# Block-sparse attention and a Fourier mixer on one core: mask matmuls regrouped and used for the second batch, late value sums and earlier q, k turned by VectorE

## The chip, the core and the metric

The kernel runs on one core of a Trainium2 chip. The metric is the time of one execution on the device in microseconds (us), lower is better. A program's time here is the median of its runs. TensorE is PE in the profile, VectorE is DVE, ScalarE is ACT, GpSimd is POOL and SyncE, which only issues transfers here, is SP. Each engine works through its own queue in order.

## What is computed

The first stage is attention with a block mask over 4 batches, 8 heads, 768 positions and head size 64; its result, laid out as (batch, position, head and feature), feeds a Fourier mixing layer with two dense products.

```python
scores = (q @ k.T) / sqrt(64)
scores = where(mask, scores, -1e9)            # 32 x 32 blocks: neighbours, first and last, 3 drawn per row
attn   = exp(scores - max) / sum
x      = (attn @ v) as (4, 768, 512)
u      = x + real(fft(fft(x, over positions), over features))
un     = (u - mean(u)) / sqrt(var(u) + 1e-6)
out    = u + relu(un @ w_ch1) @ w_ch2          # w_ch1 512 x 2048, w_ch2 2048 x 512
```

The weights arrive as 64-bit floats and are rounded to 32 bits on the chip.

## The kernel before, in words

**Units, slots, phases.** Two heads make a pair, so a batch has four pairs and the kernel sixteen, numbered n from 0. A pair has twelve units: two halves of the queries (384 each) times six chunks c of 128 keys. A slot is two units, so a pair has six slots (s from 0 to 5) and a batch 24, called a phase. `slot(sl)` at line 1240 writes out one slot by hand, and the order of the calls is the order on every queue: scores and exp of this slot's two units, values of the last slot's, then small pieces, then pieces of the mixer. There are 96 slots and one to finish.

**Scores.** `scores` (line 533) makes the scores of both heads of one unit, keys on the partitions, as two matmuls with 64 rows each, one per half of the array. In the first batch (n < NP = 4) two more matmuls with 24 rows in bf16 add the mask straight behind each unit: `of_k` says to which of the 24 blocks a key belongs, `off_q` which blocks a query may not see. In later batches the mask is a table `mask` of bytes instead, made once by matmuls in `mask_step` during phase 0.

**Exp and mask.** `weigh` (line 551) takes exp on ACT. In the first batch it writes `e` to SBUF; later it writes back to PSUM, and DVE multiplies by the mask (line 562). From the second batch on GpSimd sums the weights over the chunks into `acc` (line 572); in the first batch TensorE does it in `add_up` (line 618). Score tiles `ps_s` have two buffers, weight tiles `e` four.

**Values.** `values` (line 575) accumulates the products with v in one PSUM bank (`ps_o`, one buffer) over the six chunks of a half; ACT copies the result to `oT` (line 591, one buffer), and `place` (line 595) turns it by three TensorE transposes and lets ACT copy it into the pair's 128 columns of `x`.

**q and k.** Features must lie on the partitions. Up to pair 8 `turn` (line 469) does it with six TensorE transposes for q and six for k through the one bank `ps_t`, with ACT copies (lines 486 and 492; for pair 0's second half of q the copies are DVE's) and a square for a later range test. From pair 9 = `BY_VECTOR` on, `load_blocks` (line 214) loads 32 x 32 blocks so that block transposes of DVE (`flip_blocks`, line 511) finish the turn; ACT then puts q in order (`in_order`, line 520).

**Mixer.** `mixer` (line 872) gives, for each batch, steps that run apart (normalise, fold, Fourier products, statistics), then the late work: products in seven-multiplication form (`quad`) and second dense products (`channels`). `begin(b)` queues the batch's steps in the second slot of the next phase; `gap` issues a step where a planner with fixed costs per engine (`when`, `busy`) holds it ready; late work fills the slots, and `until` works it off where a buffer of `x` is needed again. With no late work queued, nothing but ready steps fills TensorE.

**Weights.** `w_load` and `w_round` bring 32 chunks through six rotating rooms (`room(0)` to `room(5)`) in phase 0, 1.42 chunks a slot: two ACT and five DVE instructions each.

**Small pieces.** `short` holds turns, places and sums that wait for a bank; the loop at line 1301 takes them in the slot, in phase 0 all that are ready. At the end of a slot come the DVE turns, then `load_q(n + 2)` in s = 3 and `load_k(n + 1)` in s = 0 (lines 1314 to 1317), then weights and tables.

Of the kernel before, what the change touches and what calls it, by code (L numbers as in the profile page):

```python
# [11 lines left out]
FP32 = mybir.dt.float32  # L12
# [90 lines left out]
def kernel(  # L103
# [88 lines left out]
    def busy(engine, us, after=0.0):  # L192
        when[engine] = max(when[engine], after) + us
        return when[engine]
# [14 lines left out]
    loaded, v_of = {}, {}  # L209


    BY_VECTOR = 2 * NP + 1

    def load_blocks(n, a, tile):

# [110 lines left out]
    at_k = acc_p.tile([P, 2, 2 * HS], BF16, tag="acc", name="at_k")  # L326
    at_q = acc_p.tile([P, 2, 2 * HS], BF16, tag="acc", name="at_q")
    of_k, off_q, keep_q = at_k[:, 0, :], at_q[:, 0, :], at_q[:, 1, :]

    def twice(t):  # L330
        nc.vector.tensor_copy(out=t[D:D + NB, :], in_=t[0:NB, :])
# [131 lines left out]

    turned, e_of, acc_of, o_of, sums_of, x_of, sp_of = {}, {}, {}, {}, {}, {}, {}
    s_at, e_at, oT_at, acc_at = {}, {}, {}, {}

# [61 lines left out]
    UNITS = len(pairs) * UP  # L530
    SLOT = 2

    def scores(u):
        n, w = divmod(u, UP)
        half, c = divmod(w, C)
        qT, kT = turned[n, 0], turned[n, 1]
        s = ps_s.tile([P, 2, 512], FP32, tag="s", name="s")
        busy("PE", 0.72 if n >= NP else 1.0, max(e_at.get(u - SLOT, 0.0), z_at[u % 2]))
        s_at[u] = when["PE"] + HOP
        for i in range(2):  # L540
            nc.tensor.matmul(s[:, i, 0:HS], kT[D * i:D * i + D, c * P:(c + 1) * P],  # L541
                             qT[D * i:D * i + D, half * HS:(half + 1) * HS],
                             start=True, stop=n >= NP)
        if n < NP:
            for i in range(2):
                nc.tensor.matmul(s[:, i, 0:HS], of_k[D * i:D * i + NB, c * P:(c + 1) * P],
                                 off_q[D * i:D * i + NB, half * HS:(half + 1) * HS],
                                 start=False, stop=True)
        return s

    def weigh(u, s):
        n, w = divmod(u, UP)
        half, c = divmod(w, C)
        e = ep.tile([P, 2, HS], FP32, tag="e", name="e")
        e_of[u] = e
        if n < NP:
            nc.scalar.activation(out=e, in_=s[:, :, 0:HS], func=ACT.Exp, scale=scale)
            e_at[u] = busy("ACT", 0.8, s_at[u]) + HOP
            return
        nc.scalar.activation(out=s[:, :, 0:HS], in_=s[:, :, 0:HS], func=ACT.Exp, scale=scale)  # L560
        m = mask[:, c, half * HS:(half + 1) * HS].rearrange("p (o s) -> p o s", o=1)
        nc.vector.tensor_tensor(out=e, in0=s[:, :, 0:HS], in1=m.broadcast_to([P, 2, HS]),  # L562
                                op=ALU.mult)
        e_at[u] = busy("DVE", 0.97, busy("ACT", 0.8, s_at[u]) + HOP) + HOP
        if c > 0:
            acc_at[n, half] = busy("POOL", 2.0, e_at[u]) + HOP
        if c == 1:
            acc_of[n, half] = acc_p.tile([P, 2, HS], FP32, tag="acc", name="acc")

        for i in range(2 if c > 0 else 0):  # L570
            acc = acc_of[n, half][:, i, :]
            nc.gpsimd.tensor_add(out=acc, in0=e_of[u - 1][:, i, :] if c == 1 else acc,  # L572
                                 in1=e[:, i, :])

    def values(u):
        n, w = divmod(u, UP)
        half, c = divmod(w, C)
        e = e_of[u]
        busy("PE", 0.75, e_at[u])
        vt = v_of[n]  # L580
        if c == 0:
            o_of[n, half] = ps_o.tile([P, HS], FP32, tag="o", name="o")
        o = o_of[n, half]
        for i in range(2):
            nc.tensor.matmul(o[D * i:D * i + D, :], vt[:, i, c, :], e[:, i, :],  # L585
                             start=(c == 0), stop=(c == C - 1))
        if c == C - 1:
            if half == 1:
                v_of.pop(n)
            oT = sum_p.tile([P, HS], FP32, tag="oT", name="oT")  # L590
            nc.scalar.copy(out=oT, in_=o_of.pop((n, half)))
            oT_at[n, half] = busy("ACT", 0.5, when["PE"] + HOP) + HOP
            o_of[n, half] = oT

    def place(n, half):

        b, j = pairs[n]
        oT = o_of.pop((n, half))
        if j == 0:
            x_of[b, half] = xp.tile([P, T, DM], FP32, tag=("xA", "xB")[half], name="x")  # L600
        xt, at = ps_t.tile([P, 512], FP32, tag="t", name="xt"), bank("t")
        for c in range(T):
            nc.tensor.transpose(xt[:, c * P:(c + 1) * P], oT[:, c * P:(c + 1) * P], ident)  # L603
        nc.scalar.copy(out=x_of[b, half][:, :, j * P:(j + 1) * P],
                       in_=xt[:, 0:HS].rearrange("p (c f) -> p c f", c=T))
        give(at, busy("ACT", 0.5, busy("PE", 0.45, oT_at[n, half]) + HOP))

    def into_sums(key, j, sp):
        if j == 0:
# [610 lines left out]
    def begin(b):  # L1220


        before, after, rest = mixer(b, x_of[b, 0], x_of[b, 1])
        any_of = len(late) + len(apart) + 4 * len(rest)
        hold = 2 * T
        apart.extend((*step, any_of) for step in norm_steps(b) + before)
        apart.extend((*step, hold) for step in after)
        apart.append(("-", lambda: late.extend(rest), 0.0, 0.0, 0.0, hold))

    def w_loads():  # L1230
        while state["got"] < min(len(wchunks), state["w"] + ROOMS):
# [8 lines left out]
    def slot(sl):  # L1240
# [1 line left out]
        n, s = divmod(sl, SP)  # L1242
        units = range(SLOT * sl, SLOT * sl + SLOT)
        if sl < B * SB:
            for u, ps in [(u, scores(u)) for u in units]:
                weigh(u, ps)
        if not late:
            gap(1.5)
        if 0 < sl <= B * SB:
            done = [u - SLOT for u in units]  # L1250
            for u in done:
                values(u)
            if phase == 0 or sl == SB:
                add_up(done)
            for u in done:
                e_of.pop(u)

        reuse = n % NP == 0 and phase >= 2
        if sl > 0 and s == (5 if reuse else 3) and sl <= B * SB:
            b, j = pairs[n]  # L1260
            at = oT_at[n, 0]
            if reuse:
                until(lambda: (b - 2, 0) in finished)
                at = when["PE"] + LEAVES
            short.append(("t", at, lambda: place(n, 0)))
        if 0 < sl <= B * SB and s == 0 and n % NP != 1:
            short.append(("t", oT_at[n - 1, 1], lambda: place(n - 1, 1)))
        if sl < B * SB and n % NP == 1 and s == 1:
            b = pairs[n - 1][0]
            at = oT_at[n - 1, 1]  # L1270
# [29 lines left out]

        while short and (s in (2, 5) or len(short) > 1 or phase == 0 or r == 0):
            ready = [i for i in short if max(i[1], min(free[i[0]])) <= when["PE"] + 0.1]
            if not ready and s not in (2, 5) and r > 0:
                break
            item = ready[0] if ready else short[0]
            short.remove(item)
# [1 line left out]
        if BY_VECTOR <= n + 1 < len(pairs):  # L1308
            for at, fn, args in ((0, squares, (n + 1, 0)), (1, flip_blocks, (n + 1, 0)),
                                 (2, in_order, (n + 1,)), (4, flip_blocks, (n + 1, 1)),  # L1310
                                 (5, squares, (n + 1, 1))):
                if s == at:
                    fn(*args)
        if s == 3 and n + 2 < len(pairs):
            load_q(n + 2)
        if s == 0 and 0 < n < len(pairs) - 1:
            load_k(n + 1)
        w_loads()
        w_steps(sl)
        if sl >= 4 and sl % 2 == 0:  # L1320
            table_step()

# [139 lines left out]
```

## Time and profile before

| what | us |
|---|---|
| median of 14 runs | 1110.6 |
| lowest, highest | 1106.49, 1112.19 |
| the profiled execution's own time | 1111.29 |
| its span in the trace | 1109.5 |

| phase 0 slots | from 9.3 to 136.1 us of the span |
|---|---|
| phase 1 slots | 136.1 to 253.2 |
| first batch's late work begins | about 282 |
| phases 2 and 3 | 253 to 838 |
| last batch's rest | 838 to 1109 |

The page gives busy time by engine, the span in slices, the chain of work that ended last, and groups of instructions. In a line of the timeline the first number is the start, the second the time until the last of the merged instructions ends, and x4 the number of them; matmuls overlap in the pipeline, so the cost of one is read from start to next start. A float32 matmul shows as two records, so the four records of one unit's scores are two matmuls. In the view of stretches each row has the length and then the busy time of PE, PE's weight loads, DVE, ACT and POOL, each with its count, then the granted clock of TensorE (1.00 is full), the share of the transfer engines and GB/s.

### The profile page before, as it was taken

Reading aid. Unit: us, or ns where it says so; the run is one execution under the profiler, and the core shown is the slowest. Engines: PE = TensorE matmul, PEld = TensorE weight load, DVE = VectorE, ACT = ScalarE, POOL = GpSimd, SP = SyncE. Lnnn points to the kernel's source line nnn. Section 1 sums busy time; section 2 is a strip of 40 time slices with the busy share of each in tenths; the row PEclk is TensorE's granted clock in tenths of the full one; section 3 lists DMA queues with packets and bytes.
Section 4 is the critical chain, followed back from the end, with each engine's and each line's share of the span. In section 5 each row is a group of like instructions: output and inputs, shape, how many; then the busy total and the mean of one; then the engine's idle time right before and its main releaser. Section 6 shows DMA issues by size and latency. Waiting matters only on the chain.

```text
span 1109.5 us, 12273 instructions
## 1 busy us (share of the span) xinstructions
PE 1065.7 (96%) x4370; PEld 537.9 (48%) x4370; DVE 670.8 (60%) x1227; ACT 389.6 (35%) x786; POOL 271.0 (24%) x302
## 2 busy tenths in 40 slices
PE   7999988998899999999999999999999999999996
PEld 3333333543545545444444545444444555568675
DVE  5688878497864535564558635555456446575563
ACT  4788855465202102253443112344330202120210
POOL 1000079487200001245537000343540000000000
PEclk9999999999999999999999999999999999999998
DMA  8557422022000000212210000211000000100001
GB/s 229 149 161 238 113 51 64 15 44 43 1 1 1 1 1 18 62 23 41 43 29 15 0 1 1 55 45 29 1 1 1 0 1 20 38 1 1 1 16 44
DMA packets 86689, 44.28 MB, mean 40 GB/s; under 512 B 74318, under 2 KB 79452, under 8 KB 86620
## 3 DMA queue, kind: packets, MB, share of 16 engines
q1 hardware_dynamic: 84732, 42.62, 14.6%
q10 hardware_dynamic: 1856, 0.79, 0.3%
q8 instruction: 36, 0.59, 0.2%
q14 instruction: 33, 0.27, 0.1%
q0 software_dynamic: 32, 0.01, 0.0%
HBM read 37.11 MB, written 6.29 MB: 39 GB/s over the span
## 4 chain that ended last, share of the span: by engine, by line
PE 82%; DVE 10%; ACT 2%; issue 2%; DMA 1%; POOL 1%; SPq 0%; ACTq 0%; DVEq 0%; POOLq 0%
PE y L1017 23%; PE z L961 14%; PE s L541 10%; PE o L585 8%; PE yp L961 7%; PE yy L1080 6%; PE xp L961 3%; DVE e L562 3%; PE zp L774 1%; PE sp L632 1%; PE zp L745 1%; DMA out_dram<-x 1%; PE xt L603 1%; DVE wraw L457 1%; DVE w_sb L452 1%
## 5 line engine op out<-in xcount | busy, mean ns | idle before, releaser
L572 POOL TENSOR_TENSOR acc<-acc,e 128x384 f32<-128x384 f32 x192 | 197.2, 1060 | 89.5 <-DVE e L562 88.8
L541 PE MATMUL s<-qT,kT 64*128 64x384 f32 x768 | 164.2, 531 | 15.2 <-DVE e L562 11.0
L562 DVE TENSOR_TENSOR e<-s,mask 128x768 f32<-128x768 f32 x144 | 131.1, 949 | 65.0 <-ACT s L560 63.0
L585 PE MATMUL o<-e,vr 128*64 128x384 f32 x768 | 148.2, 508 | 0.0
L560 ACT ACTIVATE s<-s 128x768 f32<-128x768 f32 x144 | 109.5, 792 | 89.2 <-PE s L541 87.8
L1020 DVE TENSOR_TENSOR x<-y,x 128x512 f32<-128x512 f32 x72 | 49.8, 692 | 146.5 <-PE y L1017 146.5
L1017 PE MATMUL y<-w_sb,hA 128*128 128x512 f32 x288 | 129.5, 596 | 1.1 <-ACT zs L776 1.1
L1017 PE MATMUL y<-w_sb,hB 128*128 128x512 f32 x288 | 128.5, 596 | 1.0 <-DVE x L1020 1.0
L572 POOL TENSOR_TENSOR acc<-e 128x384 f32<-128x384 f32 x48 | 50.0, 1062 | 232.2 <-DVE e L562 190.0
L541 PEld LDWEIGHTS s<-qT,kT 64*128 64x128 f32 x768 | 62.3, 187 | 85.1 <-DVE e L562 38.0
L966 DVE TENSOR_TENSOR hA<-z,hA 128x384 f32<-128x384 f32 x64 | 35.7, 558 | 97.4 <-PE z L961 97.4
L961 PE MATMUL z<-unT,t 128*128 128x384 f32 x256 | 93.0, 486 | 0.0
L837 POOL TENSOR_SCALAR st<-st 128x1 f32<-128x1 f32 x24 | 6.6, 276 | 348.2 <-DVE st L836 347.7
L1017 PEld LDWEIGHTS y<-w_sb,hB 128*128 128x128 f32 x288 | 53.4, 190 | 67.3 <-issue 65.6
L585 PEld LDWEIGHTS o<-e,vr 128*64 128x64 f32 x768 | 47.5, 139 | 75.9 <-issue 72.3
L1017 PEld LDWEIGHTS y<-w_sb,hA 128*128 128x128 f32 x288 | 52.9, 190 | 62.9 <-issue 58.5
L970 ACT ACTIVATE hA<-hA 128x384 f32<-128x384 f32 x64 | 33.5, 523 | 119.9 <-DVE hA L966 119.5
L961 PEld LDWEIGHTS z<-unT,t 128*128 128x128 f32 x256 | 48.7, 190 | 33.9
L970 ACT ACTIVATE hB<-hB 128x384 f32<-128x384 f32 x64 | 33.5, 523 | 86.1 <-DVE hB L966 86.1
L961 PE MATMUL xp<-unT,w_sb 128*128 128x384 f32 x128 | 48.6, 503 | 1.3 <-DVE x L1020 0.7
L981 ACT COPY hA<-xp 128x384 f32<-128x384 f32 x32 | 15.3, 478 | 95.8 <-PE xp L961 95.8
L961 PE MATMUL z<-t,w_sb 128*128 128x384 f32 x128 | 46.6, 487 | 0.9 <-DVE t L923 0.9
(197 smaller groups left out, 1409.7 us busy)
## 6 DMA issues: line engine op xcount, KB each, us to landing
wraw<-in_moe_w_ch_dram SPq DMA_DIRECT2D x32, 512.0 KB
vr<-in_v_dram SPq DMA_DIRECT2D x30, 192.0 KB
qr<-in_q_dram SPq DMA_DIRECT2D x48, 64.0 KB
kr<-in_k_dram SPq DMA_DIRECT2D x14, 192.0 KB
qb<-in_q_dram SPq DMA_DIRECT2D x28, 96.0 KB
kb<-in_k_dram SPq DMA_DIRECT2D x28, 96.0 KB
out_dram<-x SPq DMA_DIRECT2D x16, 128.0 KB
out_dram<-x SPq DMA_DIRECT2D x8, 256.0 KB
```

The source lines that it names most:

```text
L541: nc.tensor.matmul(s[:, i, 0:HS], kT[D * i:D * i + D, c * P:(c + 1) * P], qT[D * i:D * i + D, half * HS:(half + 1) * HS], start=True, stop ...
L560: nc.scalar.activation(out=s[:, :, 0:HS], in_=s[:, :, 0:HS], func=ACT.Exp, scale=scale)
L562: nc.vector.tensor_tensor(out=e, in0=s[:, :, 0:HS], in1=m.broadcast_to([P, 2, HS]), op=ALU.mult)
L572: nc.gpsimd.tensor_add(out=acc, in0=e_of[u - 1][:, i, :] if c == 1 else acc, in1=e[:, i, :])
L585: nc.tensor.matmul(o[D * i:D * i + D, :], vt[:, i, c, :], e[:, i, :], start=(c == 0), stop=(c == C - 1))
L961: nc.tensor.matmul(to, a[:, k, :], c[:, k, :], start=(k == 0), stop=(k == ND // 2 - 1))
L966: tt(out=to, in0=ps, in1=a, op=ALU.add)
L970: nc.scalar.activation(out=h, in_=h, func=ACT.Relu)
L981: nc.scalar.copy(out=h11, in_=x)
L1017: nc.tensor.matmul(y, hs[0, half][:, l, m * P:(m + 1) * P], w2_sb[:, 4 * r + l, :], start=(l == 0), stop=(l == 3))
L1020: nc.vector.tensor_tensor(out=x[:, m, :], in0=y, in1=x[:, m, :], op=ALU.add)
L1080: nc.tensor.matmul(ps, a[:, k, :], c[k // 2][:, k % 2, :] if isinstance(c, list) else c[:, k, :], start=(k == 0), stop=(k == 3))
```

## The change

Four parts.

1. `scores` takes both units of a slot: first the score matmuls of both, then the mask matmuls of both, on all 64 rows of each half of the array; the rows beyond the 24 of `of_k` and `off_q` are set to zero by two memsets.
2. Units of later batches use mask matmuls too as long as `factors["at"]` is set: `keep_factors` copies both factors by two transfers into `room(2)` in slot 21, and the step that queues the first batch's late work ends it. For these units exp writes `e`, and DVE's multiply is left out.
3. `BY_VECTOR` becomes 5, so pairs 5 to 8 are loaded in blocks and turned by DVE.
4. For pairs 9 to 11 and 13 to 15, DVE's block transpose takes the value sums from PSUM to `oT`, and sixteen transfers of 32 partitions x 3 x 32 elements put each half into `x`, with no TensorE transpose and no ACT copy.

Besides, the loads of q and k are issued earlier in their slot, and slot 1 no longer leaves its second turn (the second half of pair 0's q) to slot 2.

```diff
-    BY_VECTOR = 2 * NP + 1
+    BY_VECTOR = NP + 1
...
+    nc.vector.memset(of_k, 0.0)
+    nc.vector.memset(off_q, 0.0)
...
+    by_pe = set()
+    factors = {"at": (of_k, off_q)}
+    def keep_factors():
+        kept = room(2, [P, 2, S], "factors", BF16)
+        for a, t in enumerate(factors["at"]):
+            nc.sync.dma_start(out=kept[:, a, :], in_=t)
+        factors["at"] = kept[:, 0, :], kept[:, 1, :]
...
+    def scores(us):
+        for u in us:
+            s = ps_s.tile([P, 2, 512], FP32, tag="s", name="s")
+            if n < NP or (factors["at"] and True):
+                by_pe.add(u)
+            for i in range(2):
+                rows = slice(D * i, D * i + D)
+                nc.tensor.matmul(s[:, i, 0:HS], kT[rows, c * P:(c + 1) * P], qT[rows, queries],
+                                 start=True, stop=u not in by_pe)
+        for u, s in got:
+            if u not in by_pe:
+                continue
+            for i in range(2):
+                rows = slice(D * i, D * i + D)
+                nc.tensor.matmul(s[:, i, 0:HS], at_k[rows, c * P:(c + 1) * P], at_q[rows, queries],
+                                 start=False, stop=True)
...
     def weigh(u, s):
-        if n < NP:
+        if u in by_pe:
             nc.scalar.activation(out=e, in_=s[:, :, 0:HS], func=ACT.Exp, scale=scale)
...
     def values(u):
-            nc.scalar.copy(out=oT, in_=o_of.pop((n, half)))
+            if in_blocks(n):
+                nc.vector.transpose(out=oT, in_=o_of.pop((n, half)))
+            else:
+                nc.scalar.copy(out=oT, in_=o_of.pop((n, half)))
...
+    def in_blocks(n):
+        return n > 2 * NP and n % NP > 0
+    def place_blocks(n, half):
+        oT = o_of.pop((n, half)).rearrange("p (c t d) -> p c t d", t=P // BLK, d=BLK)
+        for g in range(P // BLK):
+            for t in range(P // BLK):
+                nc.sync.dma_start(
+                    out=x_of[b, half][BLK * t:BLK * t + BLK, :, j * P + BLK * g:j * P + BLK * (g + 1)],
+                    in_=oT[BLK * g:BLK * g + BLK, :, t, :])
...
     def begin(b):
+        def go():
+            late.extend(rest)
+            factors["at"] = None
...
     def slot(sl):
+        if s == 3 and n + 2 < len(pairs):
+            load_q(n + 2)
+        if s == 0 and 0 < n < len(pairs) - 1:
+            load_k(n + 1)
...
-            short.append(("t", at, lambda: place(n, 0)))
+            if in_blocks(n):
+                place_blocks(n, 0)
+            else:
+                short.append(("t", at, lambda: place(n, 0)))
...
-            if not ready and s not in (2, 5) and r > 0:
+            if not ready and s not in (2, 5) and r > 0 and sl > 1:
...
+        if sl == SB - 3:
+            keep_factors()
```

## The prediction

> **What bounds the kernel now.** I read the page first, then the view of stretches cut at the phases, then the waits of TensorE, then the timeline inside slots.
>
> ```profile
> PE 1065.7 (96%) x4370; PEld 537.9 (48%) x4370; DVE 670.8 (60%) x1227; ACT 389.6 (35%) x786; POOL 271.0 (24%) x302
> ...
> PE 82%; DVE 10%; ACT 2%; issue 2%; DMA 1%; POOL 1%; SPq 0%; ACTq 0%; DVEq 0%; POOLq 0%
> ```
>
> TensorE is busy 96% of the span and carries 82% of the chain that ended last. So TensorE time removed counts nearly in full where the engine is full, and elsewhere only stalls count.
>
> ```profile
> 9.00:38.00 29.00, 24.96 (x141) 8.68 (x139) 14.15 (x33) 17.01 (x33) 0.00 (x0) 0.88 0.69 206
> 38.00:136.00 98.00, 97.59 (x610) 34.66 (x606) 82.36 (x180) 80.89 (x167) 0.00 (x0) 1.00 0.58 175
> 136.00:275.00 139.00, 125.09 (x677) 54.40 (x677) 106.10 (x149) 78.94 (x166) 101.76 (x103) 0.98 0.19 43
> ...
> 450.00:838.00 388.00, 381.24 (x1484) 177.12 (x1481) 214.35 (x341) 136.27 (x259) 145.32 (x152) 1.00 0.11 24
> ```
>
> Phase 0 from 38 us on is full (97.59 of 98). The start idles 4.0 us of 29 at a mean clock of 0.88. The second batch, from 136 to 275 us, idles 13.9 us, with a lowered clock. After 450 us only 6.8 us of 388 are idle. The two idle stretches have different causes:
>
> ```profile
> PE s L541 <- DVE e L562: 9.2, 9, 2.5
> ```
>
> ```profile
> 25.25 0.55 DVE L492 COPY qT<-tp 128x128 f32<-128x128 f32 x3
> ...
> 25.95 1.65 PE L541 MATMUL s<-qT,kT 64*128 64x384 f32 x4 [4.04 <-DVE qT L492]
> ```
>
> The first line is from the waits between 136 and 275 us (total, times, longest): scores wait for DVE's mask multiply, which frees the score tile. The second pair is the start: slot 3 waits 4.04 us for three DVE copies that sat behind weight rounding.
>
> **What the Trainium skill says.** "TensorEngine Tiling (Array Packing)", Key Properties: changing the tiling mode drains TensorE. The trace agrees: a 64-row unit costs 0.85 us where 24-row masks follow and 0.745 where another 64-row unit does (below), so 0.105 a change. "TensorE: Matmul & The Clock Gate", Part 1: the clock halves after an idle window of about 3.4 us. The stretches agree roughly: mean clock 0.66 in each of 195 to 200, 253 to 258 and 280 to 285 us, that is 1.7 us lost in each, and half clock after the 4.04 us stall. "VectorE: DVE Perf Modes", the TRN2 errata: a PSUM read costs 120 cycles plus one per element. From it I estimate the new 128x384 transpose at 0.53 us; no row here shows one. "DMA: Bandwidth & Descriptors", Anatomy of one DMA: about 2 us fixed. The only landing time the page gives is 2.8 us, for the small list of sampled blocks.
>
> **Part 1, masks behind both units.** Two timelines, one slot of phase 0 and one of phase 1:
>
> ```profile
> 106.55 0.92 PE L541 MATMUL s<-qT,kT 64*128 64x384 f32 x4
> 107.40 0.34 PE L546 MATMUL s<-at_q,at_k 24*128 24x384 bf16 x2
> 107.67 0.92 PE L541 MATMUL s<-qT,kT 64*128 64x384 f32 x4
> 108.51 0.34 PE L546 MATMUL s<-at_q,at_k 24*128 24x384 bf16 x2
> 108.78 1.51 PE L585 MATMUL o<-e,vr 128*64 128x384 f32 x8
> ```
>
> ```profile
> 159.33 1.56 PE L541 MATMUL s<-qT,kT 64*128 64x384 f32 x8
> ...
> 160.82 1.51 PE L585 MATMUL o<-e,vr 128*64 128x384 f32 x8
> ```
>
> With masks a slot's scores take 108.78 - 106.55 = 2.23 us, without 1.49. A mask takes 0.265, less a 0.105 drain 0.16. In one mode throughout: 1.49 + 2 x 0.16 = 1.81, a gain of 0.42 a slot. bf16 behind float32 in one mode is not shown; if that drains as often as now, the gain is nothing, so 0 to 0.42. I take the drain as gone. Slots 4 to 23 are full: 20 x 0.42 = 8.4 us. But ACT is busy 80.89 of 98 and DVE 82.36; 8.4 us less makes both over 90% busy. I take two thirds, **5.6** (0 to 8.4).
>
> **The early turn.** Slot 1 now issues q's second half before that slot's weight rounds in DVE's queue, and ahead of them in ACT's (a square of 1.1 us). The 4.04 us and the half clock behind it (mean clock 0.57 from 24 to 32 us, so 0.43 x 8 x 2 = 6.9 us at half rate, about 5.8 of it at work: 2.9 us lost) would go. What is late next: the one turning bank, which ACT's copies of pair 1's q free at 18.2, so slot 2's scores move from 17.0 to 18.7; then unit 6's scores need unit 4's exp, now behind the square and four weight multiplies, near 23.3. That is 2.6 us ahead of 25.95, plus up to 2.9 of clock. I take **4.5** (1 to 6).
>
> **Memsets and the kept factors.** Two 128x768 memsets stand ahead of the first mask, probably partly in DVE's 1.4 us wait for the identity. The copies of the factors must wait for weight chunk 26 (DVE ends it near 122 us) and stand on SP behind `load_q(5)` (near 125); landing at 127 to 128 meets slot 22's masks at about 127. DVE no longer leads by much if TensorE speeds up. Cost **1** (0 to 3).
>
> **Part 2, the second batch's masks on TensorE.** It removes DVE multiplies and one link of the ring score, exp, multiply, value. Up to 58 of them, 52.85 us by the stretch restricted to line 562, leave DVE before 275 us. DVE's normalising and folding then come early, so Fourier products fill TensorE sooner and late work begins before slot 53. Idle to be had: 13.9 us, plus 3.1 and 0.9 us of waits for DVE up to 287 us, 17.9; clock 3 x 1.7 = 5.1. What takes its place is GpSimd:
>
> ```profile
> L572 POOL TENSOR_TENSOR acc<-acc,e 128x384 f32<-128x384 f32 x73 | 77.6, 1096 | 6.3 <-DVE e L562 6.1
> ```
>
> That is the group between 136 and 275 us: 20 adds a pair at 1.05 to 1.1 (1.05 net of overlap: 97.9 us busy over 93 adds) is 21 to 22 us. TensorE's pair would be 6 x (1.49 + 1.44 + 0.38) + 0.8 + 0.9 = 21.6. They tie where no mixer work fills, so some waiting stays: I take two thirds of both, 12.0 + 3.4 = 15.4 (8 to 21). It adds mask matmuls, 0.32 to 0.43 a slot, in 20 to 29 slots: 25 x 0.38 = 9.5 (6.5 to 12.5). They are not hidden.
>
> **Part 3, pairs 5 to 8 by DVE.** Removed: 48 transposes. Three take 0.47 us from start to start (103.38 to 103.85), so 48 x 0.157 = **7.5** of TensorE, all before 253 us. ACT loses 10.3 us of copies and gets 4 x 1.9 of reordering. DVE gets, for each pair, one of each of:
>
> ```profile
> L517 DVE STREAM_TRANSPOSE qb<-qb x7: 964/968/973, 265.2 to 766.2; 128x768 f32<-128x768 f32 x7
> ```
>
> ```profile
> L517 DVE STREAM_TRANSPOSE kT<-kb x7: 1501/1523/1544, 276.2 to 786.2; 128x768 f32<-128x768 f32 x7
> ```
>
> 4 x 2.5 = 10 us, under the 52.85 that part 2 frees. Without that cover they would stand ahead of masks, 1 us or so a pair. On SP, eight block loads at 0.524 replace six and two at 0.62 to 0.64, 0.9 us less a pair; loads stand three or four slots ahead of use, so their landing stays hidden. Parts 2 and 3 together: 15.4 - 9.5 + 7.5 = **13.4** (4 to 20).
>
> **Part 4, late sums by DVE and transfers.** Twelve halves lose three transposes each:
>
> ```profile
> 483.19 0.55 PE L603 MATMUL xt<-ident,oT 128*128 128x128 f32 x3
> ...
> 483.66 0.30 PEld L541 LDWEIGHTS s<-qT,kT 64*128 64x128 f32 x4 [0.17 <-issue]
> ```
>
> 12 x 0.47 = 5.6 us. DVE gets 12 transposes (6.4 us, where it is 55% busy); each holds the one value bank, but next to a whole slot passes before it is needed. In DVE's queue mask multiplies and channel sums stand behind it. SP gets 192 issues at about 0.33 to 0.52 us, 5 to 8 us a half, past which it brings v; the moved q and k loads go first, 2 us. Then landing: about 12 us after the sum is ready. Normalising x reads them about 9 to 11 us after the last half (line 674 at 589 and 847 us), so DVE may wait up to 3 us, twice, TensorE less thanks to late work. Net **4** (5.6 to -4).
>
> **Sum.** 5.6 + 4.5 - 1 + 13.4 + 4 = 26.5 us off the profiled execution's 1111.3 (span 1109.5, 1.8 outside) is 1084.8. That execution is 0.7 above the median, so **1084**. Within 0.2% (2.2 us) a measurement could not tell it from no change.
>
> **Rivals.** *Other engines bind*: ACT and DVE in phase 0 (83 and 84% busy), GpSimd in phase 1, so part 1 gives 2, the early turn 3, parts 2 and 3 6, part 4 3, less 1: 13 us, 1098. For it: the tie near 21.6 us. Against: averages leave room and mixer work fills. *All idle goes*: 8.4 + 6 + 20 + 5.6 = 40, 1071; for it, late work could start early enough to fill all. *Slower*: the sixteen transfers of a half go one behind another's landing. `oT` has one buffer, so the next half's DVE transpose waits, and in order behind it all mask multiplies and channel sums. The halves are 13.4 to 31 us apart by slot starts. At 1.15 us a transfer plus 4 us of loads and landing a half takes 22.4; against the spacings 19.0, 17.5, 20.0, 13.4, 17.5, 20, 14.7, 17 and 15.7 that sums to about 40 us of waiting, 1111 - 27 + 40 = 1124. It decides from about 1.05 us a transfer. Against: block loads into disjoint parts of one tile go out every 0.52 us now, without waiting.
>
> **Chances.** Forecast 0.62, by itself 1075 to 1092; other engines 0.19 (1092 to 1105); all idle 0.11 (1066 to 1075); slower 0.08. The range 1069 to 1101 leaves out the slower case and the tails. Faster 0.91, same 0.01, slower 0.08.
>
> **What would show it.** Right: scores of a phase 0 slot at 1.81 us; no 4 us gap near 22; no line 562 work from 126 to about 250 us; first late product before 260 instead of 282 us; sixteen SP issues in 8 us. Wrong: scores near 2.2; ACT or POOL as releaser of scores in the first 250 us; DVE idle before its transposes for transfers.

## The result, and the profile after

| | before | after |
|---|---|---|
| median of the runs, us | 1110.4 (47 runs) | 1117.3 (10 runs) |
| lowest, highest | 1106.5, 1112.2 | 1114.8, 1120.0 |
| the profiled execution, its span | 1111.3, 1109.5 | 1116.0, 1114.2 |

The kernel became slower by 0.7%: the ratio is 1.0070, with a 95% interval of 1.0058 to 1.0081. The forecast was 1084.

From the page after, engines and the chain that ended last:

```profile
PE 1051.0 (94%) x4370; PEld 534.1 (48%) x4370; DVE 666.9 (60%) x1207; ACT 375.3 (34%) x742; POOL 280.1 (25%) x302
...
PE 82%; DVE 8%; DMA 3%; ACT 2%; SPq 2%; issue 2%; POOL 0%; DVEq 0%; ACTq 0%; POOLq 0%
```

TensorE is busy 14.7 us less than before (1065.7); the matmuls that the prediction takes off and adds (8.4, 7.5 and 5.6 off, 9.5 more) come to 12. But the span is 4.7 us longer, so TensorE idles 19.4 us more. The same five stretches as before:

```profile
9.00:38.00 29.00, 27.44 (x182) 11.26 (x184) 18.19 (x40) 23.31 (x49) 0.00 (x0) 1.00 0.78 232
38.00:136.00 98.00, 92.93 (x615) 36.81 (x612) 84.15 (x183) 81.06 (x164) 2.62 (x3) 0.98 0.60 179
136.00:275.00 139.00, 120.44 (x629) 57.75 (x629) 82.08 (x122) 61.98 (x123) 86.83 (x86) 0.94 0.15 29
...
450.00:838.00 388.00, 369.52 (x1408) 169.24 (x1407) 220.71 (x339) 121.01 (x225) 146.32 (x151) 0.99 0.15 29
```

The start is full now (1.6 us idle instead of 4.0, clock 1.00 instead of 0.88). The stretch from 136 to 275 us, where idle time was to be won, has 18.6 us of it instead of 13.9, at a lower clock. The largest change is in the last line: 18.5 us idle where there were 6.8. The waits of TensorE after (in total, times, longest) say where:

```profile
PE s L565 <- DVE e L590: 10.0, 8, 3.1
PE s L565 <- DVE kT L532: 8.8, 1, 8.8
PE utp L935 <- ACT x L638: 6.9, 1, 6.9
PE utp L935 <- DVE sums L665: 6.3, 1, 6.3
PE s L575 <- DMA factors<-at_q: 3.4, 1, 3.4
```

The last four are single waits: for k's turn on VectorE, twice in the mixer's chain (`utp` are the transposes after normalising), and for the copied mask factors. The kernel before has none of the four; its only wait at `utp` is one of 3.1 us.

What went as foreseen is seen in a slot of phase 0 in the timeline after:

```profile
104.45 1.56 PE L565 MATMUL s<-qT,kT 64*128 64x384 f32 x8
105.84 0.49 PE L575 MATMUL s<-at_q,at_k 64*128 64x384 bf16 x4
106.27 1.51 PE L615 MATMUL o<-e,vr 128*64 128x384 f32 x8
```

A slot's scores with masks take 106.27 - 104.45 = 1.82 us; the prediction had 1.81, before it was 2.23. Both kinds of matmul use 64 rows now, and bf16 behind float32 in one mode shows no drain, which the prediction had to leave open.

### The profile page after: what moved, and what is told of

Read it like the earlier page. It is cut to its first block, busy times and chain, and to the rows that moved or that the text cites. A ratio compares the mean times of both kernels' runs of the same rounds, so it can differ in the third digit from the quotient of the medians.

```text
span 1114.2 us, 12397 instructions
## 1 busy us (share of the span) xinstructions
PE 1051.0 (94%) x4370; PEld 534.1 (48%) x4370; DVE 666.9 (60%) x1207; ACT 375.3 (34%) x742; POOL 280.1 (25%) x302
## 4 chain that ended last, share of the span: by engine, by line
PE 82%; DVE 8%; DMA 3%; ACT 2%; SPq 2%; issue 2%; POOL 0%; DVEq 0%; ACTq 0%; POOLq 0%
PE y L1066 22%; PE z L1010 15%; PE s L565 9%; PE o L615 9%; PE yp L1010 7%; PE yy L1129 6%; PE xp L1010 4%; PE zp L823 1%; SPq L653 1%; DVE x L723 1%; DMA out_dram<-x 1%; PE sp L681 1%; PE s L575 1%; PE zp L794 1%; DVE e L590 1%
## 5 line engine op out<-in xcount | busy, mean ns | idle before, releaser
L602 POOL TENSOR_TENSOR acc<-acc,e 128x384 f32<-128x384 f32 x192 | 206.1, 1105 | 99.6 <-DVE e L590 90.9
L565 PE MATMUL s<-qT,kT 64*128 64x384 f32 x768 | 155.2, 519 | 21.8 <-DVE e L590 10.0
L590 DVE TENSOR_TENSOR e<-s,mask 128x768 f32<-128x768 f32 x102 | 92.6, 947 | 51.2 <-ACT s L588 50.2
L588 ACT ACTIVATE s<-s 128x768 f32<-128x768 f32 x102 | 77.3, 789 | 127.4 <-PE s L565 126.6
L585 ACT ACTIVATE e<-s 128x768 f32<-128x768 f32 x90 | 68.0, 811 | 32.2 <-PE s L575 27.8
L1010 PE MATMUL z<-t,w_sb 128*128 128x384 f32 x128 | 46.8, 488 | 1.9 <-DVE t L972 1.9
## 6 DMA issues: line engine op xcount, KB each, us to landing
out_dram<-x SPq DMA_DIRECT2D x16, 128.0 KB
```

The source lines that it names most:

```text
L565: nc.tensor.matmul(s[:, i, 0:HS], kT[rows, c * P:(c + 1) * P], qT[rows, queries], start=True, stop=u not in by_pe)
L1010: nc.tensor.matmul(to, a[:, k, :], c[:, k, :], start=(k == 0), stop=(k == ND // 2 - 1))
```

## The experiments

The theory after reading the two traces was that part 3 puts k's turn into VectorE's queue where the mixer's chain stands (theory A in the texts below), and that part 4's transfers (theory B) or the copied factors add waits. The rival was that each part gains as forecast and that the loss is in how they act together: the order of late work, which a planner with fixed costs lays down when the program is built (theory D). All ratios are to runs of the kernel before on the same chip, four to nineteen runs a kernel. Differences in us are between medians, some of them from different chips, on which the kernel before ran at 1109.4 to 1110.8; a difference of 2 us or less is not clear of that.

**Parts left out.** Every kernel here is the changed one with one or more of three undos:

```diff
# without part 2
-            if n < NP or (factors["at"] and True):
+            if n < NP:
...
-        if sl == SB - 3:
-            keep_factors()
# without part 3
-    BY_VECTOR = NP + 1
+    BY_VECTOR = 2 * NP + 1
# without part 4
-        return n > 2 * NP and n % NP > 0
+        return False
```

Part 1, with the early turn and the earlier loads, stands in all of them.

Part 1 alone (without 2, 3 and 4):

> Only part 1 of the change (mask matmuls regrouped on 64 rows, with the memsets), the earlier second turn of slot 1 and the earlier issue of loads; masks of later batches, turns and late sums as in the kernel before. In the changed kernel's trace slot 21 starts 12.5 us earlier than in the kernel before. Both theories expect that gain to stay: 1098 us, 1094 to 1102. If it is 1106 or more, the early gain is lost later for a reason of its own (the clock, or the plan of late work), and neither theory is enough.

Parts 1 and 2:

> Parts 1 and 2: the second batch's masks are TensorE's too, q and k of pairs 5 to 8 are still turned by TensorE, late sums placed by TensorE. Theory A (the loss is k's turn standing in VectorE's queue behind mixer steps, so parts 2 and 3 together): no 8.8 us stall, only the wait for the kept factors (about 5 us with its clock) and GpSimd's limit: 1096, 1090 to 1102. Theory B (the loss is part 4's transfers): about 1093. Theory C (part 2 alone loses, since GpSimd sets the pace and the masks add 10 us): 1104 or more.

Parts 1 and 3:

> Parts 1 and 3: q and k of pairs 5 to 8 turned by VectorE, second batch's masks VectorE's multiply as before. Theory A: VectorE keeps the mask multiplies, so the plan lets few mixer steps in ahead of k's turn; but its queue is 10 us longer where TensorE waits for it: 1094 to 1102. Theory B: 1091, since 7.5 us of turns leave TensorE. If it is 1106 or more, part 3 loses by itself, without part 2.

Parts 1 and 4:

> Parts 1 and 4: late value sums by VectorE's block transposes and 192 small transfers, the rest as in the first run. Theory A: TensorE saves 5.6 us and waits some of it back: 1094 to 1099. Theory B: the transfers at 0.6 us each hold the one oT tile and VectorE behind it, and cost 10 us or more over the first run: 1106 to 1115.

Parts 1, 2 and 4:

> The change without part 3: q and k of pairs 5 to 8 stay with TensorE. If parts 2 and 4 add up, 1098.7 - 5.4 - 4.9 = 1088, and part 3 is the whole loss of the change, about 29 us (theory A, in the form: VectorE's queue, not TensorE, sets the end of the second batch). If instead parts 2 and 4 hinder each other by the shifted plan of late work (theory D), it is 1098 or more.

Parts 1, 3 and 4:

> The change without part 2: second batch's masks stay VectorE's multiply. Part 3 alone cost 9.5 us over part 1, part 4 gained 4.9, so 1103 if they add. Theory D (a plan of late work that is shifted by any change hits transfers of x): anything from 1103 to 1115.

Parts 1, 2 and 3:

> The change without part 4: 1117.3 + 4.9 = 1122 if part 4 gains in the whole change what it gained over part 1. Theory B or D (part 4's transfers of 10 us a half delay SP and VectorE in the late phases, where the changed kernel idles 18.5 us against 6.8): 1108 to 1114.

| parts | median us | lowest, highest | ratio, 95% interval |
|---|---|---|---|
| 1 | 1098.7 | 1098.0, 1099.0 | 0.990 [0.988, 0.993] |
| 1, 2 | 1093.3 | 1091.1, 1098.7 | 0.985 [0.982, 0.987] |
| 1, 3 | 1108.2 | 1106.2, 1110.7 | 0.999 [0.998, 1.000] |
| 1, 4 | 1093.8 | 1092.5, 1094.7 | 0.985 [0.983, 0.988] |
| 1, 2, 4 | 1085.9 | 1085.1, 1090.5 | 0.979 [0.977, 0.982] |
| 1, 3, 4 | 1103.4 | 1100.2, 1106.3 | 0.993 [0.991, 0.995] |
| 1, 2, 3 | 1120.6 | 1120.2, 1121.2 | 1.009 [1.007, 1.011] |
| 1, 2, 3, 4 | 1117.3 | 1114.8, 1120.0 | 1.007 [1.006, 1.008] |

Part 1 gains 10.8 us, part 2 5.4, part 4 4.9; the three together gain 24.4, a little more than the single steps add up to. Parts 1 and 4 leave the order of TensorE's mixer work as it was from slot 24 on; part 2 changes it from slot 34 on, so its gain is that of the masks and of a new order together. Part 3 loses in each pair of rows that differs in it alone: 9.5 us beside part 1, 9.6 beside 1 and 4, 27.3 beside 1 and 2, 31.4 beside all. It carries the whole loss, and it loses most where part 2 is in. The theory that part 4's transfers or part 2's masks by themselves cost the time has fallen.

Where the smallest of these losses arises is seen in the timeline of parts 1 and 3:

```profile
273.91 1.09 PE L935 MATMUL utp<-ident,un 128*128 128x128 f32 x4 [8.18 <-DVE un L898]
277.47 1.12 PE L935 MATMUL utp<-ident,un 128*128 128x128 f32 x4 [2.47 <-DVE un L898]
...
281.04 2.77 PE L1010 MATMUL xp<-unT,w_sb 128*128 128x384 f32 x4
```

Slot 53, after which the first batch's buffers of x are worked off, is reached 2.0 us earlier than with part 1 alone (260.8 against 262.8), by the transposes saved. But the mixer's chain isn't done (VectorE itself stood idle for 3.31 us of the longer wait, until GpSimd had the statistics), TensorE waits for it, and the next product runs at half clock (2.77 where the same one takes 1.46 later). Slot 54 starts at 448.3 instead of 438.4, and from there on the two stay 9.8 us apart. TensorE's idle time from slot 24 to slot 53 grows from 14.8 to 18.7 us, and in slot 53 from 5.0 to 12.7: the transposes had been filling time in which little else was ready. From slot 52 on the mixer work has the same order in both kernels, so this loss is not one of the order of late work. Between slots 37 and 51 the order differs, and whether that or the longer queue made the chain late was not tested.

**VectorE's time or the plan.** Part 3 gives VectorE about 2.5 us a pair and changes what the planner is told. Three kernels without part 3 take the two apart. The first and second have VectorE make two idle transposes a pair into an unused room (for pairs 5 to 7, and for pair 8 while the first batch's late work has not begun: seven and six in all), with and without telling the planner; the third tells the planner alone. The first kernel has all these lines, the second leaves the last one out, the third has only the condition and the last one. None changes the output.

```diff
+        if NP < n + 1 < BY_VECTOR and factors["at"] and s in (1, 4):
+            idle = room(3, [P, S], "idle")
+            nc.vector.transpose(out=_at(idle, 0, [(1, P), (P, C)]) if s == 4 else idle,
+                                in_=turned[n, 0])
+            busy("DVE", 1.0)
```

> As the run without part 3 (TensorE turns q and k), but VectorE also does block transposes of the same size at the same places for pairs 5 to 7 (8 only while late work has not begun), into a tile that nobody reads; that work is added, the output is the same. If VectorE's time and queue are what part 3 costs, this is slower than the run without part 3 by 3 us or more. If what costs is that scores wait for the turned k behind mixer steps, it is within 2 us of the run without part 3.

> The run with idle block transposes (1113.9 us), but the planner is not told of them, so every queue has the order of the run without part 3 (1085.9), with VectorE's added transposes in it. That work is added, the output is the same. If the transposes' own time is the loss, about 1110; if the loss is the shifted plan, 1087 to 1093 (they are 2.5 us a pair, three pairs at most).

> The opposite: the planner is charged 1 us of VectorE at the same places, and no transpose is added. If the shifted plan is the loss, about 1108 to 1113; if VectorE's time is, 1086 to 1089.

| added to parts 1, 2, 4 (1085.9) | median us | ratio, 95% interval |
|---|---|---|
| transposes, planner told | 1113.9 | 1.004 [1.003, 1.006] |
| transposes, planner not told | 1088.8 | 0.981 [0.979, 0.982] |
| planner told, no transposes | 1111.9 | 1.003 [1.001, 1.004] |

The transposes cost 3 us, which is not clear of nothing (the intervals, 0.979 to 0.982 here and 0.977 to 0.982 without them, overlap). Two microseconds a pair in the planner's books cost 26, with not one instruction added. Untold, the order is that of parts 1, 2 and 4 throughout. From slot 34 on TensorE's scores and mixer work stand in the two told kernels in the very order of the full change. So they do in the next kernel, the full change with VectorE's turns of pairs 5 to 8 left out of the books:

```diff
         nc.vector.transpose(out=out, in_=t)
-        busy("DVE", 1.0)
+        if n > 2 * NP:
+            busy("DVE", 1.0)
```

> The whole change, with the planner not told of VectorE's turns of pairs 5 to 8. If the shifted plan is the greater part of the loss, the plan comes near that of the run without part 3 and the time to 1095 to 1105, with the 8.8 us wait for the turned k still there. If VectorE's real queue is, it stays at 1115 to 1122.

It took 1121.9 us (1.010 [1.008, 1.012]). Not charging VectorE doesn't bring the old order back: from slot 34 on it is that of the full change. TensorE's charges for the turns are gone in it and ScalarE's are different, and that too is enough to tip the planner.

**The factors' copies.** In the full change TensorE waits in slot 22 for the copied factors. TensorE and then SP's queue, after:

```profile
113.33 1.61 PE L565 MATMUL s<-qT,kT 64*128 64x384 f32 x8 [0.36 <-ACT e L585]
118.33 0.59 PE L575 MATMUL s<-factors 64*128 64x384 bf16 x4 [3.39 <-DMA factors<-at_q]
```

```profile
110.32 3.11 SPq L222 DMA_DIRECT2D qb<-in_q_dram  x4
113.53 0.53 SPq L478 DMA_DIRECT2D factors<-at_k  x1
114.09 0.60 SPq L478 DMA_DIRECT2D factors<-at_q  x1
```

The copies stand behind q's loads, are issued at 113.53 and 114.09, and the second, 4 us later, lets the masks go. The slot takes 10.20 us instead of the 5.05 it takes with part 1 alone, without the wait. An amendment of the kernel without part 3 issues them one slot earlier, and uses them from slot 24 on only:

```diff
-        if sl == SB - 3:
-            keep_factors()
+        if sl == SB - 4:
+            factors["kept"] = keep_factors()
+        if sl == SB - 1:
+            factors["at"] = factors["kept"]
```

(`keep_factors` returns the two copies instead of setting them.)

> The change without part 3, with the two factor transfers issued one slot earlier and used only from slot 24 on. The 3.4 us wait in slot 22 and the half clock behind it go: 1085.9 - 3.4 - 1.7 = 1081, 1079 to 1083. If the time stays at 1085, the wait was covered by something else.

It took 1082.0 us (0.976 [0.974, 0.978]), 3.9 less than without the amendment; in the profiled executions slot 24 starts at 122.3 instead of 126.4 us, with no half clock after slot 22 in either.

**Cover and queue.** Two waits of the full change had a story each. The 6.94 us before `utp` come late, in slot 81:

```profile
717.08 1.78 PE L565 MATMUL s<-qT,kT 64*128 64x384 f32 x8 [0.47 <-DVE e L590]
725.79 1.11 PE L935 MATMUL utp<-ident,un 128*128 128x128 f32 x4 [6.94 <-ACT x L638]
726.84 2.83 PE L615 MATMUL o<-e,vr 128*64 128x384 f32 x8
```

There the late work of the batch before had run out (slots 80 to 88 hold none of it), and the next batch's sums wait until stores have landed and x is free (ScalarE's copy into `x` waits 9.67 us for `out_dram<-x`). The planner holds back `COVER` = 100 us of late work for this. The story: too little of it. The 8.78 us wait is for k, in VectorE's queue after, with TensorE below it:

```profile
137.09 0.98 DVE L532 STREAM_TRANSPOSE qb<-qb 128x768 f32<-128x768 f32 x1
...
139.88 7.87 DVE L723 TENSOR_TENSOR x<-x,r 128x512 f32<-128x512 f32 x6
147.78 2.43 DVE L746 TENSOR_TENSOR sa<-x 128x1536 f32<-128x1536 f32 x1
150.14 2.54 DVE L746 TENSOR_TENSOR sd<-x 128x1536 f32<-128x1536 f32 x1
152.61 1.74 DVE L750 TENSOR_TENSOR sa<-sa 128x765 f32<-128x765 f32 x1
...
157.49 1.50 DVE L532 STREAM_TRANSPOSE kT<-kb 128x768 f32<-128x768 f32 x1
```

```profile
148.84 1.51 PE L615 MATMUL o<-e,vr 128*64 128x384 f32 x8
159.13 2.93 PE L565 MATMUL s<-qT,kT 64*128 64x384 f32 x8 [8.78 <-DVE kT L532]
161.82 0.88 PE L575 MATMUL s<-factors 64*128 64x384 bf16 x4
```

The mixer's chain (normalise, fold) holds VectorE without a break from 139.88, and k's turn of pair 5 is in the middle of it. TensorE, with no other work queued, waits and then runs at half rate: a slot's score matmuls take 2.93 us instead of 1.56. "TensorE: Matmul & The Clock Gate", Part 1, in the Trainium skill names a free-running window of about 3.4 us of idling for that. The clock granted in these traces agrees with a window of that length: apart from the end of the span, half clock comes in stretches of 3.41 us or a multiple of it (at the waits of 8.78 and 6.94 us it lasts 10.24 and 6.83). The traces don't agree with 3.4 us as the least wait. After the wait of 3.39 us above the masks took 0.59 us and the transposes next 0.90 (0.55 at full clock), while parts 1, 2 and 4, with 3.38 us at the same place, went on at full clock, and so did the control below after 3.66 us. In the kernel before, waits of 2.48, 2.17 and 3.09 us stand at the three stretches of half clock in which the prediction saw rough agreement. So for waits of 2 to 4 us it seems to depend on where the window lies.

Four kernels test the stories, in this order: the full change with more cover; with k's turn earlier; with both and the early copies; and, as a control, parts 1, 2 and 4 with the early copies and more cover.

```diff
# the first, third and fourth
-    COVER = 100.0
+    COVER = 115.0
# the second and third
-                                 (2, in_order, (n + 1,)), (4, flip_blocks, (n + 1, 1)),
+                                 (2, in_order, (n + 1,)), (2, flip_blocks, (n + 1, 1)),
```

The full change with more cover:

> The change as given, but the planner holds back 115 us instead of 100 us of late work as cover for the next batch's mixer chain. If the loss sits late in the span (cover that runs out, slots 80 to 88 with no late work and the wait for the stores), some 13 us of it go: about 1104. If cover isn't the cause: 1117, as the change.

The full change with k's turn earlier:

> The change as given, but VectorE's turn of k is put into its queue at a pair's third slot instead of the fifth, ahead of that pair's mixer steps. If the turn's place in VectorE's queue is a cost of its own, the 8.8 us wait of slot 30 and its half clock go: about 1105, and as much as 1100 if slot 35's wait goes too. If the queue only shifts: 1115 or more.

The full change with both, and the early copies:

> The change with three amendments: 115 us of cover, k's turn at a pair's third slot, and the copies of the mask factors issued four slots before the end of the first batch and used two slots later. If plan and queue are together the loss: 1085 to 1090, near the change without its third part. If the turn on VectorE costs in itself: 1100 or more.

The early copies and more cover, without part 3:

> The control to the two runs with 115 us of cover: the change without its third part, with the early copies of the factors, and 115 us of cover. There the cover did not run out, so 1081 to 1084, no more than 2 us from the same kernel with 100 us; a gain of more would say that cover helps every version and not this loss.

| kernel | median us | ratio, 95% interval |
|---|---|---|
| full, more cover | 1118.8 | 1.007 [1.005, 1.010] |
| full, k earlier | 1111.2 | 1.002 [1.000, 1.003] |
| full, both and early copies | 1102.1 | 0.992 [0.990, 0.995] |
| without part 3, early copies, more cover | 1101.4 | 0.992 [0.990, 0.994] |

The cover story fell. More cover does take the 6.94 us wait away, but others come in its place, and in the control, which was not to move by more than 2 us, it costs 19.4. There the planner puts a whole seven-multiplication piece into slot 73 with nothing beside it, and its products wait for VectorE, from the timeline of that control:

```profile
548.99 1.46 PE L1010 MATMUL z<-t,t 128*128 128x384 f32 x4
556.48 2.93 PE L1010 MATMUL z<-unT,t 128*128 128x384 f32 x4 [6.04 <-DVE hA L1015]
```

k's turn put earlier is worth 6.1 us, half of what the story asked; the order of TensorE's mixer work is the same up to slot 84. And with the early copies and more cover the kernels with and without part 3 are level (1102.1 and 1101.4); from slot 49 on they have the same order. That pointed to the order and away from part 3's own cost.

**The order held.** The last two kernels have all four parts, and the planner is charged for pairs 5 to 8 (counted from 0; the first text below counts from 1) as if TensorE still turned them. TensorE's sequence is then that of the kernel without part 3, and of the one with early copies, matmul by matmul, less the 48 transposes. The planner's order is that of every queue, so what these kernels hold is not TensorE's order alone.

```diff
+    def turn_plan(n, a, half):
+        at = bank("t")
+        done = busy("PE", 0.15 * (2 if a == 0 and half else 4 if a == 0 else T)) + HOP
...
+                elif s == at and n + 1 <= 2 * NP:
+                    short.append(("t", 0.0, lambda a=a, half=half: turn_plan(n + 1, a, half)))
```

(`turn_plan` goes on with ACT's charges as `turn` has them, and issues nothing. The charges of `squares`, `flip_blocks` and `in_order` are left out for these pairs. The second kernel adds k's earlier turn and the early copies.)

> The change as given, with all its turns on VectorE, but the planner is charged for pairs 6 to 9 as if TensorE still turned them, so that TensorE's order is exactly that of the change without its third part (1085.9) less the 48 transposes. If the order of the late work makes most of the 31 us: about 1095 (1085.9, 7.5 of transposes off, some 15 of waits for k and of half clock after them on). If waits behind VectorE make most of it: 1110 or more.

> The same, with k's turn at a pair's third slot and the factors' copies two slots early; TensorE's order is exactly that of the run e12 (1082.0) less the 48 transposes. If order and queue are all of the third part's loss: 1078, in a range of 1074 to 1083, and the third part gains for once. If turns on VectorE cost more than they save on TensorE even so: 1085 or more.

| | without part 3 | with part 3, same order | with part 3, planner's own order |
|---|---|---|---|
| as given | 1085.9 | 1089.0 [0.979, 0.982] | 1117.3 |
| k earlier, early copies | 1082.0 | 1082.8 [0.973, 0.977] | not run at 100 us of cover |

(In brackets the 95% interval of the ratio to before.) With the order held, the loss of 31.4 us shrinks to 3.1, and that isn't clear of nothing: the interval without part 3 is 0.977 to 0.982. The waits of TensorE with the order held, as given:

```profile
PE s L581 <- DVE kT L546: 10.4, 1, 10.4
PE s L581 <- DVE e L606: 3.8, 3, 1.7
PE s L591 <- DMA factors<-at_q: 3.5, 1, 3.5
```

and with k earlier and the early copies:

```profile
PE zp L810 <- DVE sa L783: 8.6, 1, 8.6
PE s L581 <- DVE e L606: 4.2, 4, 1.8
```

The wait for k is there in full, even longer. Put earlier, it goes, and the mixer's first products wait for `sa` instead, 8.6 us where it is 3.7 without part 3: VectorE's queue is the limit there, and what is put ahead pushes the rest back.

Slot by slot, from the starts of score matmuls in the timelines (us):

| | slot 24 | slot 53 | slot 54 | slot 78 | slot 95 | span |
|---|---|---|---|---|---|---|
| parts 1, 2, 4 | 126.4 | 324.8 | 428.7 | 679.1 | 796.9 | 1083.3 |
| full, order held | 129.6 | 329.1 | 433.0 | 683.2 | 801.0 | 1087.4 |
| full | 128.0 | 332.7 | 444.0 | 692.9 | 819.0 | 1114.2 |

Of the 4.1 us by which the second row is late, 3.2 are there at slot 24, before pair 5: half clock after a wait for the factors that both have (3.50 and 3.38 us, with half clock after the first alone). That is luck of the window and no cost of part 3. From slot 25 to the end part 3 costs 0.9. Against the first row the full change is 7.9 us late at slot 53, 15.3 at slot 54, 22.1 at slot 95 and 30.9 at the end: it also leaves one seven-multiplication piece more for the time after the last slot.

## Why the prediction was wrong

**Part 1 and the early turn: right.** 5.6 + 4.5 = 10.1 us was forecast for the two; 10.8 were measured. The scores of a slot are 1.82 us (forecast 1.81), the 4.04 us wait in slot 3 is gone. With part 1 alone slot 4 starts 6.8 us earlier than before (26.2 against 33.0) and slots 4 to 23 take another 6.8 us less, so phase 1 starts at 122.5 instead of 136.1 us. Both terms were taken too small, the second because ACT and VectorE would bind; that their sum came out is in part luck, since some of the 13.6 us went again later.

**The kept factors: the mechanism right, the size too small.** 1 us (0 to 3) was taken; 3.9 were measured beside parts 1, 2 and 4, and in the held order, where half clock follows, slot 24 comes 6.6 us later than with early copies. The prediction had the copies issued near 125 us and landed at 127 to 128, when the masks come; the second copy let the masks go 4.2 us after its issue.

**Part 2: right, with an open end.** 15.4 - 9.5 = 5.9 was forecast, 5.4 measured (7.9 beside part 4). In the profiles of parts 1, 2 and 4 against 1 and 4, TensorE idles 21.1 us instead of 29.0, with the new wait for the factors in it, and its mean clock is 0.997 instead of 0.989, 7 to 8 us by an estimate from the span. The masks are in 19 slots instead of 25, 8.2 us at 0.43 a slot (an estimate). The late work begins in slot 42 instead of 53, as foreseen. How good the planner's new order would be was not foreseen, and how much of the 5.4 it makes was not tested.

**Part 4: right.** 4 was forecast, 4.9 measured, with the order of TensorE's mixer work unchanged. The slower rival's mechanism did not appear (by the spacings that the prediction gives, its waits sum to 46.8 us and not to about 40). From the group of one tile, after:

```profile
L653 SPq DMA_DIRECT2D x<-oT x192: 585/597/1344, 476.9 to 843.0; - x192
...
L622 DVE STREAM_TRANSPOSE oT<-o x12: 550/573/583, 476.3 to 832.7; 128x384 f32<-128x384 f32 x12
...
  DMA x<-oT: 2.7, 2
```

A transfer is issued every 0.60 us, not over 1.05; the turn takes 0.573 us (the prediction's estimate was 0.53); VectorE waited for the buffer twice, 2.7 us in all. The rival's end, slower than before, came about by something else.

**Part 3: the step that failed.** It said 7.5 us of TensorE for 48 transposes, and "4 x 2.5 = 10 us, under the 52.85 that part 2 frees. Without that cover they would stand ahead of masks, 1 us or so a pair." Two things are wrong in it.

The small one is that cover. The 52.85 us are freed as a sum over the stretch, not where k's turn stands. What is queued ahead of it isn't mask multiplies but the mixer's chain, 17.6 us of VectorE in one piece (139.88 to 157.49), and part 2 took nothing off that. The turns do take 8.9 us out of TensorE's slots between pairs 5 and 8 (about 6.6 of matmuls and 2.2 of waits for the turning bank, slot by slot against parts 1, 2 and 4); the wait for k, its half clock and smaller waits, less one of 3.6 that goes, take 9.9 back. So with the order held part 3 is worth about nothing, not 7.5. Without part 2, where the prediction had a cost of 1 us or so a pair, it loses 9.5 us though the late work keeps its order: in slot 53 TensorE waits for the mixer's chain, and time saved on TensorE before that is lost.

The large one was no term of the sum at all. The planner lays the order down from its own costs, and part 3 changes these: 48 transposes off TensorE's books, 2 us a pair on VectorE's. That this moves work was not priced. It makes 1117.3 - 1089.0 = 28.3 of the 31.4 us, shown by holding the order and, from the other side, by changing the books alone (26 us). The kernel as changed and the one in the held order have the same work but for the masks of two slots, which TensorE adds in the first (21 slots of the second batch against 19, since late work begins later). In the first TensorE idles 51.2 us between its first and last matmul, in the second 27.8: 4.3 more in slots 24 to 43, 5.9 in slots 44 to 57, 2.0 in slots 65 to 79 and 10.7 in slots 80 to 88. The largest in slots 24 to 43 is the wait of 6.3 us for VectorE's sums in slot 39. In slots 44 to 57 and 65 to 79 seven-multiplication pieces stand alone in a slot and wait for VectorE, or slots have no late work, where the held order mostly has channel products; in slots 80 to 88 there is no late work at all, where the held order has two pieces and four channel products. TensorE is also busy 3.4 us longer, in part for those masks, the rest at half clock after the waits.

The prediction's signs of being right nearly all came true in the slower kernel: scores at 1.82 us, no 4 us gap near 22, no mask multiply on VectorE before 257.1 us, the first late product at 241.9 instead of 282.2. (Sixteen issues take 9.6 us, not 8.) Two of its signs of being wrong showed and were small: ScalarE as releaser of scores (2.6 us in four waits) and VectorE waiting for the transfers (2.7 us). None of the signs looks at part 3's own term or at the order.

Why the planner's order without part 3 is so much better isn't settled. Among the kernels with parts 2 and 4 three orders of the mixer's work were seen: one at 1082 to 1089 us in five kernels, with or without part 3; one at 1111 to 1122, the same at least from slot 34 to slot 83, in five; and one with 115 us of cover, the same from slot 49 on, at 1101 to 1119 in three. (Parts 1, 2 and parts 1, 2, 3 have the first and the second but for the place of a sum or two.) Whether a change of books lands in the good one was not predictable from the profile of before.

Without part 3 the forecast would have been 1111.3 - 19 = 1092; 1085.9 were measured. The fastest kernels found are parts 1, 2 and 4 with early copies of the factors (1082.0) and the full change in the held order (1082.8). They can't be told apart.

## What to carry to other kernels

When an order of instructions comes from a cost model, moving work between engines changes the model's input, and the new order can be worth more than the work moved: here 28 us against the 7.5 that had been forecast. Ask for it when you forecast, and, when you test, hold the order (charge the old costs, issue the new instructions) before you blame an engine. And write down, for every term of the sum, a sign that would show it wrong. Time freed on an engine is cover only where it lies: look at what stands in that engine's queue ahead of the moved instruction, at the moment when someone waits for it.

## What the runs showed of the hardware

VectorE and GpSimd slow each other down. Normalising x takes 1.31 us an instruction in phase 1 and 0.65 at the end. VectorE and then GpSimd, after:

```profile
139.88 7.87 DVE L723 TENSOR_TENSOR x<-x,r 128x512 f32<-128x512 f32 x6
...
847.23 1.29 DVE L723 TENSOR_TENSOR x<-x,r 128x512 f32<-128x512 f32 x2
```

```profile
137.24 7.14 POOL L602 TENSOR_TENSOR acc<-acc,e 128x384 f32<-128x384 f32 x6
144.35 2.85 POOL L602 TENSOR_TENSOR acc<-e 128x384 f32<-128x384 f32 x2
147.16 3.91 POOL L602 TENSOR_TENSOR acc<-acc,e 128x384 f32<-128x384 f32 x2
```

In the first case GpSimd adds without a break, in the second it has nothing to do. The Trainium skill ("SBUF — State Buffer", SBUF: two separate sides) says that a VectorE instruction with two SBUF inputs and a GpSimd instruction that reads SBUF lock each other out for the whole instruction. The trace nearly agrees: from 140.6 to 146.3 us each engine starts one instruction every 1.41 us, where VectorE starts one every 0.60 at the end and GpSimd one every 0.96 just before, together 1.56. The mask multiplies, which read one input from PSUM, show none of it: they take 0.91 to 0.96 us throughout. From 139.88 to 157.49 the chain ahead of k's turn takes 17.6 us; the same instructions at the end of the kernel add up to about 9.4. By this estimate GpSimd's additions may be the larger part of the 8.78 us that TensorE waits for k; no run without them tests it.
